# Score products and two weight heads moved in front of a data-dependent branch, with the first rows of maxima loaded there

## The chip, the core and the metric

The kernel runs on one core of a Trainium2 chip. The core has a matrix engine (TensorE, PE in the profile), a vector engine (VectorE, DVE), an activation engine (ScalarE, ACT), a general engine (GpSimd, POOL) and an engine that mostly issues transfers (SyncE, SP), besides 16 DMA engines. Each engine works through its own queue of instructions in order, and semaphores hold an instruction back until its inputs are there. The metric is the device time of one execution in microseconds (us).

## The reference

The input is layer-normalised once; an attention with 32 heads of 16 and one shared key and value head (A), and a layer of experts chosen by product keys (B), are added to the input.

```python
x = A_x                                   # 1 x 2048 x 512
xn = _layernorm(x, axis=-1)
# A
q = (xn @ wq).reshape(B, S, 32, 16).transpose(0, 2, 1, 3)
k, v = xn @ wk, xn @ wv
p = softmax(einsum("bhqd,bkd->bhqk", q, k) * 16 ** -0.5)
a = einsum("bhqk,bkd->bhqd", p, v) ... @ wo
# B: 32 heads, 64 x 64 experts, two of them per head and token
s1 = einsum("nhd,ed->nhe", q1, k1); s2 = einsum("nhd,ed->nhe", q2, k2)
# the best 2 of each, the best 2 of their 4 sums, softmax g over these
act = gelu(einsum("nd,nhkd->nhk", xn, u[top_e]))
b = einsum("nhk,nhk,nhkd->nd", g, act, v[top_e])
return x + a + b
```

## The kernel before, in words

**Tiles.** The 2048 tokens are 16 tiles of 128, in four groups of four. For the experts a "chunk" is four of the 32 heads: its score product for one tile of tokens is a 128x512 result of twelve matmuls over four slices of the model dimension and three terms of a split of both operands into a high and a low part (`item`, line 531). Eight maxima (line 544) and eight index searches (line 546) on VectorE follow for each such item. Four items are a batch; `batch` works out the gates on VectorE and ScalarE and the expert numbers on GpSimd (lines 590 to 606).

**Weights of a chunk.** `wp_make(c)` forms the folded weights of a chunk: one step for each of four heads (load of `wqt`, line 471; a few matmuls, line 487; a copy on ScalarE, line 488), then four steps of transposes (line 494) with a high part from ScalarE (line 496) and a low part from VectorE (line 497).

**One thread of score work.** `score_thread` yields the whole score work in small steps, each with a cost in us: 0.9 for a head, 0.45 for a slice of transposes, 0.705 for three matmuls of an item. `run_scores(until=...)` runs steps until the account `spent` reaches a value, `run_scores(key=...)` until the expert numbers of one item exist. Chunk 0's weights are 4 x 0.9 + 4 x 0.45 = 5.4 in this account.

**Gathers.** `gather` fetches, for one slot of 128 tokens, the rows of both expert tables by an indirect transfer from GpSimd's queue (line 987) into one of twelve buffers (`NGB`). `dot` (line 999) then forms the activation on VectorE, and `add` (line 1034) adds the weighted row to the sum of the tile. A buffer is free again after its `add`.

**The start.** Group after group is normalised (`norm_group`, with a square root on ScalarE, line 154), transposed (`transpose_group`, lines 182 to 187), projected to keys and values (`project_kv`) and to queries (`project_q`, lines 229 to 241, twelve matmuls for each of four slices, the results stored to memory by SP). Here the framework's own scheduler orders each engine's instructions: the order in the code is a priority, and what is ready may go ahead. Between the key projection of group 1 and the rest stand the weights and the four items of chunk 0 with their maxima, and then `flush`, which runs the deferred work (the exponential of the gates, line 583, among it). The first six gathers stand after group 2's keys, the next six after group 3's.

**The guard.** `guard` (lines 252 to 267) bounds the scores of the attention from the largest squared norms of queries and keys: a few small operations on VectorE, two one-column transposes on TensorE (`pm`, line 258), and a flag (line 264). Every engine loads the flag (line 265) and branches on it (line 266). Only if the bound is exceeded does `true_maxima` run, which works out the real maxima into the memory tensor `d_m`; with these inputs it does not, and `d_m` holds the zeros that `zero_m` wrote.

**The loop.** Behind it, 256 steps and some more run with an order written out by hand for all engines (`manual_schedule`). A step `d` takes two key blocks of an attention unit: scores (line 327), exponentials (line 330), products with the values (line 341). In `mid` come dots, sums and deferred work, in `fill` score steps up to the target `aim`, which rises from `done0`, the account at the loop's start, to 948 in equal shares. `pos` counts how many dots should have been formed; it starts at 0.0 and grows by 2.1 in the first steps and by other rates later, and in the last quarter by what is left divided by the steps that are left. `load_q(u)` loads a unit's query rows (lines 317 to 319) and, with `maxima`, its two rows from `d_m` (line 314). In the very first step `load_q(0, rows=False)` loads the rows of maxima for unit 0, behind the branch, and `run_scores(until=spent[0] + 1.8)` starts chunk 1's weights.

The calls of the start are at the bottom of the kernel (lines 1203 to 1260).

Of the kernel before, what the change touches and what calls it, by code (L numbers as in the profile page):

```python
# [40 lines left out]
NGB = 12  # L41
# [14 lines left out]
def tile_kernel(ctx, tc, x, wq, wkv, wo, wqT, kT, uv, ub, vb, out):  # L56
# [194 lines left out]
    def guard():  # L251

        mm = small.tile([P, 2], F32, name="mm", bufs=1)
        nc.vector.reduce_max(mm[:, 0:1], qmax, axis=AX.X)
        nc.vector.reduce_max(mm[:, 1:2], ksq_p, axis=AX.X)
        p = xtile("pm")
        for i in range(2):
            nc.tensor.transpose(p[:1, i * P:(i + 1) * P], mm[:, i:i + 1], ident)
        m2 = small.tile([1, 2], F32, name="m2", bufs=1)
        nc.vector.reduce_max(m2, p[:1, :2 * P].rearrange("p (a n) -> p a n", a=2), axis=AX.X)  # L260
        pr = small.tile([1, 1], F32, name="prd", bufs=1)
        nc.vector.tensor_mul(pr, m2[:, 0:1], m2[:, 1:2])
        fl = small.tile([1, 1], I32, name="flag", bufs=1)
        nc.vector.tensor_scalar(fl, pr, LIMIT2, None, op0=OP.is_gt)
        flag = nc.values_load(fl[0:1, 0:1], min_val=0, max_val=1)
        with tc.If(flag != 0):
            true_maxima()

    def true_maxima():
        ptile = lambda dt, shape: late[0].tile(list(shape), dt, name="mx", tag="pt", bufs=6)  # L270
# [34 lines left out]
    def load_q(u, rows=True, maxima=True):  # L305
        qb, hg = units[u]
        qa = qa_bufs[u % 2]
        QA[u] = qa
        c = slice(qb * 512, (qb + 1) * 512)
        for b in range(2):  # L310
            h0 = 4 * hg + 2 * b
            o = 64 * b
            if maxima:
                nc.sync.dma_start(raw(qa[o + 48:o + 50]), d_m[:, h0:h0 + 2, c])
            if rows:
                src = [d[h0 * DH:(h0 + 2) * DH, c].rearrange("(h r) n -> r h n", r=DH) for d in (d_qh, d_ql)]
                nc.sync.dma_start(raw(qa[o:o + 16]), src[0])
                nc.sync.dma_start(raw(qa[o + 16:o + 32]), src[0])
                nc.sync.dma_start(raw(qa[o + 32:o + 48]), src[1])
# [756 lines left out]
    def posts():  # L1076
        while POST:
            for fn in POST.pop(0):
                fn()
# [48 lines left out]
    spent = [0.0]  # L1128

    def run_scores(until=None, key=None):  # L1130
        while (until is not None and spent[0] < until) or (key is not None and key not in IDX):
            posts()
            try:
                cost = next(sgen)
            except StopIteration:
                spent[0] = 1e9
                posts()
                return
            if cost is None:

                if key is None:
                    return
                continue
            spent[0] += cost
# [4 lines left out]
    def att_steps(d, mid, fill):  # L1149
        i = 2 * d  # L1150
        run(STORES)
        if 144 <= i < STEPS and i % 128 == 16:
            PWO.extend((i // 128 - 1, j) for j in range(4))
        if i < STEPS:
            u, kc = divmod(i, 16)
            if i == 0:
                load_q(0, rows=False)
                run_scores(until=spent[0] + 1.8)
            if kc == 4 and u + 1 < 32:
                load_q(u + 1)  # L1160
            scores(u, kc, 0)
            scores(u, kc, 1)
        if 0 < i <= STEPS:
            pu, pk = divmod(i - 2, 16)
            pv(pu, pk)
            pv(pu, pk + 1)
            if pk == 14:
                unit_tail(pu)
        mid()
        if i < STEPS:  # L1170
            scores(u, kc + 1, 0)
            scores(u, kc + 1, 1)
        if out_ready() and (i % 128 >= HOLD and PWO[0][0] != 1 or i % 128 >= 32 and i % 4 == 0 and PWO[0][0] == 1):
            block_out()
            spent[0] += 3.6
        fill()

        pp, r = divmod(i, 32)
        if pp and pp < 16:
            if r == 4:  # L1180
                pair_load(pp - 1)
            if r == 6:
                pair_invert(pp - 1)
            if r == 10:
                pair_spread(pp - 1)
            if r == 12:
                pair_tail(pp - 1)
        if i == STEPS - 4:
            for j in range(3):
                last_out_a(j)  # L1190
        if i == STEPS + 2:
            last_out_a(3)
            last_out_b()
        if i >= 124 and i % 128 == 124 or i == STEPS - 30:
            lent[0] = 2
        if 128 <= i < STEPS and i % 128 == (26 if i // 128 == 2 else 10) or i == STEPS - 10:
            load_wo()
        if i == STEPS - 6:
            load_last()
# [29 lines left out]
    for base in (48, 112):  # L1229
        nc.scalar.dma_start(raw(kaug[base:base + 2, :]).rearrange("r (i n) -> r i n", n=512),  # L1230
                            ones_f[:, None, :].to_broadcast([2, 4, 512]))
    run_scores(key=(0, 0, 3))
    flush()
    zero_m()
    norm_group(2, xs[2])
# [1 line left out]
    transpose_group(2)  # L1237
    project_kv(2)
    xs.append([load_x(3 * GT + j, False) for j in range(GT)])
    gathers(NGB // 2)  # L1240
    project_q(2, wqs)
    norm_group(3, xs[3])
    transpose_group(3)
    project_kv(3)
    gathers(NGB // 2)
    project_q(3, wqs)
    run(STORES)
    start_stack.close()
    wp_load(1, 0)
    wp_load(1, 1)  # L1250
    late[0] = pool("late", bufs=1)
    load_q(0, maxima=False)
    guard()
    E_ = mybir.EngineType
    with tc.manual_schedule(engines={E_.PE, E_.Activation, E_.DVE, E_.Pool, E_.SP}):
        done0 = spent[0]
        half = STEPS // 2
        pos, since = 0.0, half
        for d in range(half + 24):


            if dense_on[0] != 0:
                since = d
            if dense_on[0] == 1:
                pos += 2.6 if d < half * 3 // 4 else max(0.0, NSL - pos) / max(half - 3 - d, 1)
            else:
                pos += (2.1 if len(IDX) < NC * TPH else 2.3 if 0 <= d - since < 12 else 1.75, 0, 1.4, 1.5, 0.5)[dense_on[0]]

            todo = max(min(int(pos + 0.001), g_next[0]) - d_next[0], 0)

            def mid():
                post = POST[:]
                POST.clear()
                for act, _ in post:
                    act()
                tanhs(d_next[0])
                run(ON_ACT)
                ON_ACT.extend(LATER_ACT)
                LATER_ACT.clear()
                run(LAST)  # L1280
                LAST.extend(LATER)
                LATER.clear()
                rest = BEHIND[:]
                BEHIND.clear()

                dots(d_next[0] + todo - 1)
                if a_ready[0] > a_next[0]:
                    weigh(a_next[0] // SB)
                dots(d_next[0] + 1 if todo > 0 else 0)
                for _, fn in post:  # L1290
                    fn()
                sums = min(a_ready[0] - a_next[0], max(todo, 3) if d < half else 4)
                if dense_on[0] > 2:
                    sums = min(sums, 2)
                if quiet[0] > 0:
                    quiet[0] -= 1
                    sums = 0
                if dense_on[0] == 2:
                    run(CHAIN)

                def go():
                    n = sums
                    while rest or CHAIN or n > 0:
                        if n > 0:
                            adds(1)
                            n -= 1
                        elif not rest:
                            run(CHAIN)
                        if CHAIN:
                            CHAIN.pop(0)()  # L1310
                        if rest:
                            rest.pop(0)()
                    gathers(4)

                    for _ in range(1 if d < half - 4 else NT):
                        if OUTS:
                            experts_out(OUTS.pop(0))

                if dense_on[0] == 2:
                    POST_FILL.append(go)  # L1320
                else:
                    go()

            aim = done0 + (FILL - done0) * (d + 1) / half if d < half else 1e6

            def fill():
                run_scores(until=min(aim, spent[0] + MOST))
                run(POST_FILL)

            att_steps(d, mid, fill)  # L1330
        flush()
        run(STORES)
        while a_next[0] < NSL:
            dots(NSL)
            run(CHAIN)
            tanhs(d_next[0])
            adds(SB)
            run(STORES)
            gathers(NGB)
        assert not OUTS  # L1340
        run(STORES)
# [37 lines left out]
```

## Time and profile before

| what | value |
|---|---|
| median of three runs | 1915.05 us (1909.74 to 1916.33) |
| the profiled execution's own time | 1918.82 us |
| its span in the trace | 1917.1 us |
| granted clock of TensorE, mean | 0.985 |
| bytes read and written in memory | 426.49 MB and 55.61 MB |
| transfers by indirect gathers | 268.47 MB in 73728 packets |
| first two score products of the loop | from 139.21 us |

The span is divided into 40 slices of about 48 us; a digit gives the busy share of a slice in tenths (9 is 90% or more), and the row PEclk the granted clock in tenths. A row of the timeline has the start and length in us, engine and line, what is written from what, how often, and in brackets the idle time before it with what ended that. Rows whose engine ends in q are those of a queue, not of its engine. The profile does not count a register load, a branch or an issued transfer as busy time.

### The profile page before, as it was taken

The numbers are of one execution on the slowest core, as the hardware profiler recorded it, in microseconds if no ns is written. First come the engines' busy times: TensorE is split into PE (matmuls) and PEld (weight loads), VectorE is DVE, ScalarE is ACT, GpSimd is POOL, SyncE is SP. The second block draws the span as 40 slices with busy tenths as digits, with TensorE's granted clock in tenths as the row PEclk, the third lists the DMA queues.
The fourth block names the chain that finished last, engine by engine and source line by source line (L and its number), as shares of the span: only waits on it lengthen the run. The fifth ranks groups of instructions, "written<-read, shape, count | busy, mean of one in ns | idle before, by whom it ended". The sixth has DMA issues, their size and how long they took to land.

```text
span 1917.1 us, 35007 instructions
## 1 busy us (share of the span) xinstructions
PE 1822.9 (95%) x10990; PEld 961.5 (50%) x10990; DVE 1633.0 (85%) x6381; ACT 1290.6 (67%) x1803; POOL 693.8 (36%) x920
## 2 busy tenths in 40 slices
PE   6879999999999889999999999999998899999998
PEld 4544444555555344555555454555543345555553
DVE  6626888889998987999999797899989779999994
ACT  3236666655557987787877555555579777878773
POOL 1202334334443213343444354344522124444430
PEclk9989999999999999999999999999999899999999
DMA  7856878898673678898999987877646878899982
GB/s 264 312 191 235 293 267 289 286 296 282 232 261 111 223 245 259 250 288 274 284 289 307 340 283 234 290 244 264 229 129 220 263 222 292 267 285 280 295 265 79
DMA packets 245724, 489.76 MB, mean 255 GB/s; under 512 B 93972, under 2 KB 106644, under 8 KB 245532
## 3 DMA queue, kind: packets, MB, share of 16 engines
q0 software_dynamic: 73728, 268.47, 42.1%
q1 hardware_dynamic: 170568, 218.18, 35.0%
q8 instruction: 88, 1.44, 0.3%
q10 hardware_dynamic: 1236, 0.82, 0.1%
q14 instruction: 104, 0.85, 0.1%
HBM read 426.49 MB, written 55.61 MB: 251 GB/s over the span
## 4 chain that ended last, share of the span: by engine, by line
PE 76%; DVE 10%; DMA 3%; ACT 2%; issue 1%; SPq 1%; ACTq 0%; DVEq 0%
PE pv L341 20%; PE psc L531 18%; PE sc L327 15%; PE pact L733 9%; PE pout L872 9%; DVE oh L792 3%; PE pwo L434 2%; DVE xa L1034 2%; DVE g L999 1%; PE pw L487 1%; DVE oh L795 1%; ACT pt L330 1%; DVE oh L794 1%; DMA wqt<-in_wqT_dram 1%; DMA wk<-dw 1%
## 5 line engine op out<-in xcount | busy, mean ns | idle before, releaser
L330 ACT ACTIVATE pt<-sc 128x1024 f32<-128x1024 f32 x1024 | 994.6, 1028 | 449.1 <-PE sc L327 394.2
L987 POOL DMA_INDIRECT g<-in_uv_dram,idx x512 | 555.0, 1084 | 997.1 <-DVE xa L1034 518.3
L341 PE MATMUL pv<-pt,vaug 128*32 128x512 f32 x4096 | 499.4, 604 | 0.0
L327 PE MATMUL sc<-qa,kaug 64*128 64x512 f32 x2048 | 387.7, 451 | 15.7 <-ACT pt L330 14.1
L531 PE MATMUL psc<-wk,xt 128*128 128x512 f32 x1536 | 390.4, 402 | 8.0 <-DMA wk<-dw 4.4
L1034 DVE SCALAR_TENSOR_TENSOR xa<-g,w,xa 128x512 f32<-128x512 f32 x512 | 372.2, 745 | 0.1
L999 DVE CUSTOM_DVE_ANT_0 g<-g,xa 128x512 f32<-128x512 f32 x512 | 335.7, 682 | 6.2 <-DMA g<-in_uv_dram,idx 6.2
L531 PEld LDWEIGHTS psc<-wk,xt 128*128 128x128 f32 x1536 | 278.9, 189 | 111.8 <-issue 39.6
L327 PEld LDWEIGHTS sc<-qa,kaug 64*128 64x128 f32 x2048 | 157.4, 186 | 332.3 <-ACT pt L330 206.5
L341 PEld LDWEIGHTS pv<-pt,vaug 128*32 128x32 f32 x4096 | 107.7, 110 | 247.6 <-issue 246.0
L546 DVE FIND_INDEX8 i<-m,psc 128x8 uint32<-128x64 f32 x1024 | 206.6, 222 | 0.0
L733 PE MATMUL pact<-xt,wk 128*128 128x512 f32 x768 | 196.0, 400 | 0.0
L872 PE MATMUL pout<-wk,wd 128*128 128x512 f32 x768 | 194.9, 402 | 0.2 <-DVE wd L930 0.2
L544 DVE MAX8 m<-psc 128x8 f32<-128x64 f32 x1024 | 146.6, 215 | 41.3 <-PE psc L531 36.8
L872 PEld LDWEIGHTS pout<-wk,wd 128*128 128x128 f32 x768 | 140.8, 188 | 47.5 <-DVE act L999 5.5
L733 PEld LDWEIGHTS pact<-xt,wk 128*128 128x128 f32 x768 | 139.4, 188 | 48.5 <-issue 17.4
L875 DVE TENSOR_TENSOR da<-da,pout 128x512 f32<-128x512 f32 x128 | 82.9, 680 | 10.1 <-PE pout L872 6.6
L698 DVE TENSOR_TENSOR wk<-rw,wk 128x512 fp32r<-128x512 f32 x128 | 84.9, 684 | 6.7 <-ACT wk L697 6.7
L792 DVE TENSOR_TENSOR oh<-oh 128x2048 f16<-128x2048 f16 x64 | 78.0, 1219 | 0.6 <-ACT pt L330 0.4
L697 ACT CAST wk<-rw 128x512 fp32r<-128x512 f32 x128 | 74.1, 632 | 0.0
L546 DVE MATCH_VALUE_LOAD i<-m,psc 128x8 f32 x1024 | 72.6, 71 | 0.0
L1022 DVE SCALAR_TENSOR_TENSOR w<-gth,ga 128x4 f32<-128x4 f32 x128 | 20.5, 160 | 51.2 <-ACT gth L1015 50.6
(159 smaller groups left out, 1344.6 us busy)
## 6 DMA issues: line engine op xcount, KB each, us to landing
wk<-dw SPq DMA_DIRECT2D x96, 512.0 KB
wqt<-in_wqT_dram SPq DMA_DIRECT2D x32, 512.0 KB
dw<-wk SPq DMA_DIRECT2D x32, 512.0 KB
rw<-in_ub_dram SPq DMA_DIRECT2D x64, 256.0 KB
rw<-in_vb_dram SPq DMA_DIRECT2D x64, 256.0 KB
gy<-dg SPq DMA_DIRECT2D x64, 256.0 KB
qa<-dqh SPq DMA_DIRECT2D x128, 64.0 KB
g<-in_uv_dram,idx POOLq DMA_INDIRECT x512
```

The lines of the kernel that those rows point to most:

```text
L327: nc.tensor.matmul(p[:, b, :], kaug[o:o + 64, kc * P:(kc + 1) * P], QA[u][o:o + 64, i, :], start=True, stop=True)
L330: nc.scalar.activation(pt, p, AF.Exp, scale=SCALE)
L341: nc.tensor.matmul(PV[u][32 * j:32 * j + 32, :], vaug[:, kc, :], pt[:, b, :], start=kc == 0, stop=kc == 15)
L531: nc.tensor.matmul(p, XT[k][:, a, j * P:(j + 1) * P], WC[n_][k][:, bb, :], start=n == 0, stop=n == 11)
L544: nc.vector.max(m8[:, jb, s, :], p[:, s * E:(s + 1) * E])
L546: nc.vector.max_index(i8[:, jb, s, :], m8[:, jb, s, :], p[:, s * E:(s + 1) * E])
L733: nc.tensor.matmul(p, us[:, a, k * P:(k + 1) * P], XT[k][:, c, :], start=n == 0, stop=n == 11)
L792: nc.vector.tensor_tensor(out=oa, in0=num(P), in1=bc(0, tb, P), op=OP.is_equal)
L872: nc.tensor.matmul(p, wd[0][:, a, j * P:(j + 1) * P], vs[:, c, :], start=n == 0, stop=n == 5)
L987: nc.gpsimd.indirect_dma_start(out=gt, out_offset=None, in_=uv, in_offset=bass.IndirectOffsetOnAxis(ap=IDX[ph, c, ti][:, s:s + 1], axis=0))
L999: nc.vector.tensor_tensor_reduce(u, u, XN[TPH * ph + ti], scale=1.0, scalar=0.0, op0=OP.mult, op1=OP.add, accum_out=a[:, i:i + 1])
L1034: nc.vector.scalar_tensor_tensor(acc, v, w[:, i:i + 1], acc, op0=OP.mult, op1=OP.add)
```

## The change

Four items of chunk 0 leave their place after group 1's keys; there, `run_scores(until=5.3)` now stops when chunk 0's weights are made. The items, their deferred work, all twelve gathers and the first heads of chunk 1's weights stand in `guard`, after the flag has been computed and ahead of the load of it. `load_q(0)` loads the rows of maxima along with the query rows ahead of the guard; where the branch is taken, they are loaded again behind `true_maxima`. The first loop step no longer does either, and `pos` starts at -2.1.

```diff
@@ guard
         nc.vector.tensor_scalar(fl, pr, LIMIT2, None, op0=OP.is_gt)
+        run_scores(key=(0, 0, 3))
+        flush()
+        gathers(NGB)
+        run_scores(until=spent[0] + 1.8)
         flag = nc.values_load(fl[0:1, 0:1], min_val=0, max_val=1)
         with tc.If(flag != 0):
             true_maxima()
+            load_q(0, rows=False)
@@ att_steps
             u, kc = divmod(i, 16)
-            if i == 0:
-                load_q(0, rows=False)
-                run_scores(until=spent[0] + 1.8)
             if kc == 4 and u + 1 < 32:
@@ the start
-    run_scores(key=(0, 0, 3))
+    run_scores(until=5.3)
     flush()
...
-    gathers(NGB // 2)
     project_q(2, wqs)
...
     project_kv(3)
-    gathers(NGB // 2)
     project_q(3, wqs)
...
-    load_q(0, maxima=False)
+    load_q(0)
     guard()
...
-        pos, since = 0.0, half
+        pos, since = -2.1, half
```

## The prediction

> **What bounds the kernel now.** I read the page's first two parts, then the start stage by stage, because the diff touches only what stands around the branch ahead of the attention loop.
>
> ```profile
> span 1917.1 us, 35007 instructions
> PE 1822.9 (95%) x10990; PEld 961.5 (50%) x10990; DVE 1633.0 (85%) x6381; ACT 1290.6 (67%) x1803; POOL 693.8 (36%) x920
> ...
> PE   6879999999999889999999999999998899999998
> ...
> PEclk9989999999999999999999999999999899999999
> ```
>
> TensorE is busy 95% of the span and has its loose slices at the very start. So time can only come out of places where TensorE waits, and those are here (the windows view; columns are length, busy time of each engine with instruction counts, granted clock, DMA share):
>
> ```profile
> 52.20:63.15 10.95, 10.95 (x50) 9.02 (x49) 9.07 (x74) 0.55 (x1) 0.00 (x0) 1.00 0.74 281
> 63.15:76.69 13.54, 10.49 (x44) 7.27 (x42) 10.16 (x55) 6.80 (x11) 8.02 (x16) 1.00 0.76 257
> 76.69:104.30 27.61, 21.66 (x85) 13.79 (x85) 10.20 (x20) 6.39 (x12) 5.52 (x6) 0.88 0.86 335
> 104.30:124.73 20.43, 19.18 (x87) 12.46 (x86) 8.48 (x14) 7.98 (x15) 0.00 (x0) 1.00 0.61 226
> 124.73:133.72 8.99, 0.96 (x4) 0.09 (x3) 2.24 (x6) 0.94 (x2) 0.00 (x0) 0.63 0.26 90
> 133.72:139.21 5.49, 4.68 (x13) 1.09 (x14) 0.00 (x0) 1.17 (x2) 0.00 (x0) 0.68 0.64 222
> 139.21:147.42 8.21, 5.45 (x22) 2.05 (x20) 0.42 (x1) 7.12 (x9) 0.00 (x0) 0.80 0.37 111
> ...
> 139.21:1917.10 1777.89, 1718.81 (x10558) 895.74 (x10556) 1559.73 (x6133) 1248.69 (x1728) 672.26 (x875) 0.99 0.78 255
> ```
>
> The first row is chunk 0's score products, the second the rest of query projection 1, the third all of group 2, the fourth all of group 3, the fifth the guard with its branch, the sixth the first heads of chunk 1's weights, the seventh the first loop step. Groups 2 and 3 do the same work, yet group 2 takes 7.18 us more (27.61 against 20.43). The guard has 0.96 us of TensorE work in 8.99. From the first loop score (139.21) on, TensorE is busy 1718.81 of 1777.89 us, so the loop keeps nearly all of what it gets early or late: a shift of the first score is a shift of the end.
>
> Now the timeline of group 2 (start, length, instruction, and in brackets the idle time before it and what released it):
>
> ```profile
> 66.16 0.32 POOL L590 CAST fi<-i 128x64 f32<-128x64 uint32 x1 [57.50 <-DVE i L546]
> ...
> 68.79 1.28 ACT L583 ACT_TABLE_LOAD   x1
> 68.92 1.16 POOL L987 DMA_INDIRECT g<-in_uv_dram,idx  x1 [0.29 <-POOL idx L606]
> ...
> 72.51 1.28 ACT L154 ACT_TABLE_LOAD   x1
> ...
> 74.39 0.69 DVE L999 CUSTOM_DVE_ANT_0 g<-g,xa 128x512 f32<-128x512 f32 x1 [3.00 <-DMA g<-in_uv_dram,idx]
> ...
> 76.38 0.38 PE L237 MATMUL pqs<-qsq,blk 128*32 128x512 bf16 x1 [1.83 <-DVE act L999]
> ...
> 82.66 0.69 DVE L241 TENSOR_REDUCE qmax<-pqs 128x1 f32<-128x512 f32 x1 [3.03 <-remote]
> 82.80 0.94 POOL L987 DMA_INDIRECT g<-in_uv_dram,idx  x1 [0.30 <-remote]
> 86.17 1.07 ACT L183 CAST xtt<-ptr 128x512 fp32r<-128x512 f32 x2 [6.77 <-remote]
> ...
> 86.81 1.36 PE L200 MATMUL pkv<-xtt,wkv_h 128*32 128x512 f32 x2 [4.91 <-ACT xtt L183]
> ```
>
> The twelve gathers are issued from 68.92 to 83.74. While they fill the DMA engines, ScalarE stands still for 6.77 us and VectorE for 3.03 us, released by something that the view calls only "remote", and TensorE loses 4.91 us waiting for ScalarE. After it the matmuls are slow (1.36 us for two), so the clock adds to it. Nothing like it is in group 3, which has no gathers. Two loop dots (line 999) ran at 74.39 although the code has them behind the branch: outside the written order the framework's scheduler lets work cross the branch.
>
> The guard itself:
>
> ```profile
> 126.48 0.38 PE L237 MATMUL pqs<-qsq,blk 128*32 128x512 bf16 x1 [1.75 <-ACT qsq L236]
> 127.83 0.58 PE L258 MATMUL pm<-ident,mm 128*1 128x128 f32 x2 [0.98 <-DVE mm L254]
> 129.09 0.14 DVE L264 TENSOR_SCALAR flag<-prd 1x1 int32<-1x1 f32 x1
> ```
>
> What its two lines did in each queue (duration in ns as least, median, most, then first and last start):
>
> ```profile
> L265 PEldq TENSOR_LOAD <-flag x1: 492/492/492, 129.3 to 129.3; - x1
> L266 POOLq COMPARE_BRANCH  x1: 45/45/45, 129.8 to 129.8; - x1
> L266 PEldq COMPARE_BRANCH  x1: 3568/3568/3568, 129.9 to 129.9; - x1
> ```
>
> The weight heads before and behind it, again in the timeline:
>
> ```profile
> 45.41 3.65 PE L487 MATMUL pw<-wqt,kTs 128*64 128x512 f32 x14
> ...
> 133.75 3.67 PE L487 MATMUL pw<-wqt,kTs 128*64 128x512 f32 x8 [5.33 <-PEq L266]
> ...
> 134.39 5.28 SPq L471 DMA_DIRECT2D wqt<-in_wqT_dram  x4
> ...
> 138.20 1.08 PE L487 MATMUL pw<-wqt,kTs 128*64 128x512 f32 x4 [0.78 <-PE pw L487]
> ...
> 139.92 1.28 ACT L330 ACT_TABLE_LOAD   x1
> ```
>
> The flag is written at 129.23. TensorE's queue loads it (0.49 us), spends 3.57 us in the branch and starts again at 133.72: 4.49 us. Then come three heads (twelve matmuls; four make a head), not the two that the step of 1.8 names, since the sum of costs falls a rounding short of its bound.
>
> **The change part by part.** Negative is saved time on the path to the first score.
>
> a. Chunk 0's 48 score matmuls leave the stretch 52.20 to 63.15 and come back behind group 3. They cost 10.95 us in either place: 0 by themselves. VectorE's 32 maxima and 32 index searches move along; an item's round is 60.62 minus 57.90, 2.72 us, against 10.95/4 = 2.74 us on TensorE, so they keep pace and end one item behind.
>
> ```profile
> 57.90 1.15 DVE L544 MAX8 m<-psc 128x8 f32<-128x64 f32 x8
> ...
> 60.62 1.15 DVE L544 MAX8 m<-psc 128x8 f32<-128x64 f32 x8
> ```
>
> b. Query projection 1 loses the dots, the searches on VectorE and the two table loads (68.79 and 72.51) between its steps. Its stretch idles 13.54 minus 10.49 = 3.05 us; group 3's idles 1.25. Saving between 0 and 3.05; I take 1.5, near the difference of 1.8.
>
> c. Group 2 without the gathers: between 0 (the stall has another cause) and 7.18 (it becomes group 3). I take 6, near group 3, because the stall starts and ends with the burst.
>
> d. The flag's latency, 124.73 to 129.23, is 4.50 us with 0.96 us of work; the score products fill the 3.5. Between 0 (they are put elsewhere) and 3.5; I take 3.5, for 10.95 us are ample cover and wait for nothing here.
>
> e. The three heads cost 5.49 us behind the branch, with half the clock and SP's loads (134.39) queued behind the branch. In front of it, at the rate of 45.41, they cost 12 x 3.65/14 = 3.1: saving 2.4 at most, 0 at worst. The loads are hidden under the score products. If that cover is gone, the third head waits as at 138.20. I take 2.4.
>
> f. TensorE's load and branch stay: the same 4.3 us (0.49, 3.57 and the step after), now behind the heads instead of behind the flag. I take 0; at worst the fetch meets the burst, below.
>
> g. The exponential's table is loaded for chunk 0's gates in front of the branch and no square root comes after it, so the load at 139.92 is gone: between 0 and 1.3; I take 1.3. The maxima rows' two small transfers leave SP's queue behind the branch and cost nothing in front of it, under the score products.
>
> h. The twelve gathers now start when the indices of chunk 0 are there: after VectorE's last item and POOL's chain of 2.76 us (66.16 to 68.92), some 5.5 us behind the last product, while TensorE is in its branch. POOL's own branch stands behind them. The first rows are there 74.39 minus 68.92 = 5.5 us later, and the start position of -2.1 gives the first step no dots, so the dots of the second step, about 8.2 us on (seventh row), find their rows. What can be lost is the stall of c, at its new place: 0 to 7.18. I take 2.5: nearer to 0, since DMA share there is 0.37, where the stall met 0.86.
>
> i. VectorE leaves its branch later, so chunk 1's weight halves come later: 0 to 2.7 (one item); I take 0.5. The two dots that move into the loop meet an idle VectorE (0.42 of 8.21 us busy) and cost 0; the schedule spreads the rest of the lag over its last quarter. The cost account begins 2.7 higher and changes only how the fill is spread.
>
> Sum: -1.5 - 6 - 3.5 - 2.4 - 1.3 + 2.5 + 0.5 = -11.7 us. From the profiled execution's 1918.8 us (its span of 1917.1 and 1.7 around it) that is 1907.1. The three runs shown have a median of 1915.05, 3.8 lower, so on their footing the forecast is **1903.4**.
>
> A page of the Trainium skill speaks against a part of this: "TensorE: Matmul & The Clock Gate", section "Part 1: The HAM clock gate (the "warmup" mystery)", has the array go to half its clock after about 3.4 us idle and need as long of work to come back. The clocks of 0.63 and 0.68 in the fifth and sixth row agree. By it the branch's gap still leaves a cold array, now in front of the scores: half of 3.4 us, 1.7, would be lost of e, as an estimate from that page, and the sum would be -10.0.
>
> **The rivals.** *The burst only moves.* The stall of c turns up behind the branch with its whole price: the sum has +7.2 in place of +2.5, -7.0 in all, and 1908.1. For it: the same twelve transfers, and several engines leaving a branch at that moment. Against it: loop steps all have gathers, and they run nearly without TensorE waiting.
> Of the Trainium skill, "Runtime: NRT & Kernel Launch", section "Instruction fetch mechanics", says that a taken branch to code not yet held must fetch it by DMA; by that rule the branch and the burst compete for the same engines. The branch's 3.57 us agree, though no row shows that fetch under load.
>
> *The order does not change as written.* The scheduler let dots cross the branch; it can also pull products and gathers forward into the gaps of groups 2 and 3. Then b, c and d are not had, h costs nothing, and e and g remain: -3.7, 1911.4. Against it: the code's order is its priority, and projections fill TensorE in groups 2 and 3 (19.18 of 20.43).
>
> *The branch is a meeting point (slower).* If no engine can leave the branch before all have entered it, TensorE waits for POOL, which stands behind twelve gathers. Counted from the last product: 2.7 (VectorE's item), 2.8 (index chain), 14.8 (68.92 to 83.74) make 20.3, against 3.1 for the heads: 17.2 us more. Then the sum is -14.7 + 0.5 + 17.2 = +3.0, and +9.0 if group 2's stall also stays; its middle, +6, gives 1921.1. It decides once the wait exceeds 14.2 us. For it: the present trace has all engines idle at the branch, so it could not show. Against it: each queue has its own load and its own branch of 45 ns, TensorE's alone being long.
>
> **How the numbers follow.** Forecast 0.60, with a range of its own from 1897 (every saving whole and no loss: 3.05 + 7.18 + 3.5 + 2.4 + 1.3 = 17.4) to 1909; the burst only moves 0.12; order unchanged 0.12; meeting point 0.16. A measurement of this kernel can tell about 0.3% from no change, 5.7 us: 1909.3 to 1920.8. Faster: 0.60 of the forecast, less its slow edge, with two thirds of the second, a little of the third, about 0.70; same 0.14; slower 0.16. The range reaches over the second and third case and leaves out the meeting point: 1895 to 1914.
>
> **What would show it.** Group 2's stretch near 20.4 us without a "remote" wait; line 531's first 48 products between the last projection and line 266; ScalarE with two table loads in the start instead of four; twelve line 487 matmuls ahead of the branch; the first score near 126 us; TensorE still about 4 us in the branch; from there to the end the same 1778 us. I would be wrong if the gathers come before the guard in the trace, if TensorE's branch lasts as long as POOL's gathers, or if the stretch behind the first score grows by more than the first score is earlier.

## The result: the first score came 9.2 us earlier, and the end 18 us later

The changed kernel takes 1932.01 us (median of six runs, 1927.93 to 1937.30), the kernel before 1914.28 us (six runs, 1909.74 to 1918.59): a ratio of 1.0098, 95% interval 1.0079 to 1.0117. (Here and below the ratio is estimated from all runs of both kernels; it is not quite the quotient of the two medians.) It is slower by 17.7 us; 1903.4 us, a gain of 11.7, was forecast. Line numbers of the changed kernel are 5 higher behind the guard, those of e12 below 6.

The page of the changed kernel, parts 1 and 2:

```profile
span 1927.9 us, 34996 instructions
...
PE 1823.1 (95%) x10990; PEld 962.0 (50%) x10990; DVE 1632.9 (85%) x6381; ACT 1289.7 (67%) x1801; POOL 686.9 (36%) x920
...
PE   6979999999998889999999899999988899999998
...
PEclk9989999999999999999999899999999999999999
```

TensorE does the same work in the same busy time (1823.1 against 1822.9 us). What grew is its idle time, and the digits show no place for it at the start: new eights stand in the later slices.

The windows view of the changed kernel's start, cut at the same events as in the prediction (rest of query projection 1 with the last transposes of the weights, group 2, group 3, the flag's latency, chunk 0's products, heads and branch, the first loop step):

```profile
52.10:65.91 13.81, 13.80 (x64) 9.96 (x64) 6.89 (x12) 6.29 (x11) 0.00 (x0) 1.00 0.52 173
65.91:85.23 19.32, 18.57 (x85) 12.49 (x84) 11.38 (x26) 6.87 (x13) 0.00 (x0) 1.00 0.64 238
85.23:105.65 20.42, 19.45 (x87) 12.47 (x86) 8.58 (x14) 8.09 (x15) 0.00 (x0) 1.00 0.66 251
105.65:108.98 3.33, 0.51 (x3) 0.14 (x3) 1.54 (x3) 0.94 (x2) 0.00 (x0) 1.00 0.98 376
108.98:121.67 12.69, 12.69 (x51) 10.05 (x49) 8.77 (x75) 0.00 (x0) 0.00 (x0) 0.87 0.88 286
121.67:129.98 8.31, 2.84 (x13) 0.71 (x13) 4.26 (x34) 3.14 (x5) 4.10 (x12) 0.98 0.36 103
129.98:140.35 10.37, 8.91 (x35) 4.43 (x35) 1.98 (x3) 6.10 (x8) 7.93 (x9) 0.68 0.97 342
```

The first score is at 129.98 instead of 139.21. But from there to the end of the span it is 1927.9 - 130.0 = 1797.9 us, against 1777.9 before:

```profile
129.98:1927.90 1797.92, 1720.53 (x10556) 896.26 (x10556) 1560.31 (x6137) 1248.30 (x1726) 674.90 (x885) 0.99 0.78 255
```

Twenty microseconds were lost behind the part that the change moved. This is the last of the signs of being wrong that the prediction had named: the stretch behind the first score grew by more than the first score is earlier.

The 9.2 us come from one pair of executions, and the start varies. In the six kernels whose start is that of before (before, e4, e5, e11, e13 and e14 below) the first score comes at 135.2 to 139.2 us, in the changed kernel and e1, e7, e8 and e10, which have its start, at 128.3 to 130.2. On average it is 8.0 us earlier.

To find where, the start of the first exponential of each loop step was read from both traces (the instructions of line 330 and line 335 in order of time, four to a step). The first column is its time in the profile of before in us, the others are the difference to it: the changed kernel, and five kernels of the experiments below.

```
step   before   changed    e1     e7     e4     e11     e5
   0    141.2    -10.2   -11.1  -10.0   -1.7   -0.8   -3.4
   1    147.1     -2.9   -10.4   -9.5   +2.6   -2.9   -2.7
   6    184.5     -0.7    -9.8   -9.2   +2.3   +4.7   -2.6
  28    351.1     -4.3    -7.7   -9.8   -1.2   +9.4   -1.0
  64    600.3     +0.0    -8.0  -10.1   +1.2  +10.7   -1.1
  76    666.7     +1.2    -2.9  -10.1   +4.8  +15.0   +3.6
 104    854.8     +6.6    -3.5   -9.8  +11.9  +12.6   +3.3
 132   1051.6     +6.7    -3.0   -9.9  +11.2  +12.6   +5.5
 140   1112.6    +10.8    -5.9  -11.0  +14.3  +16.6   +6.2
 188   1440.7     +9.4    -6.0  -11.1  +12.7  +21.3   +6.6
 200   1507.3     +9.7    -1.2  -12.0  +13.3  +19.8  +10.6
 255   1894.8    +12.2    +0.8  -13.1  +13.5  +18.1  +11.8
```

The profiled execution of before lies above the median of its runs (1918.8 against 1914.28 us), and its first score is the latest of the six equal starts, so all columns flatter the other kernels by a few us; how a column changes from row to row is what counts. In the changed kernel's column the lead of 10.2 us shrinks to 2.9 within the first step, is gone by step 64, and turns into a lag of 6.6 by step 104 and of 10.8 at step 140. The experts of two of the four token groups are not gathered but worked out by matmuls over all experts with one-hot rows (lines 825, 733 and 872); a stretch of steps in which these run is called a dense phase here. In the trace of before the first fills steps 63 to 134 and the second steps 181 to 253. Steps 64 to 104 lie in the first, and steps 132 to 140 hold its end.

The largest wait of TensorE in the loop is there. The timeline of the changed kernel around it, of SP, VectorE and TensorE (rows picked):

```profile
1050.71 1.69 SPq L510 DMA_DIRECT2D wk<-dw  x2
...
1053.07 0.59 SPq L379 DMA_DIRECT2D rc<-dsum  x1
...
1068.25 0.35 DVE L384 RECIPROCAL rc<-rc 128x32 f32<-128x32 f32 x1 [9.78 <-DMA rc<-dsum]
...
1071.78 2.13 PE L877 MATMUL pout<-wk,wd 128*128 128x512 f32 x4 [8.78 <-DVE wd L935]
```

The same transfers in the timeline of the kernel before:

```profile
1046.82 0.32 SPq L374 DMA_DIRECT2D rc<-dsum  x1
...
1049.16 0.91 SPq L505 DMA_DIRECT2D wk<-dw  x2
```

Before, the small load of a pair's softmax sums (16 KB) was issued ahead of the next chunk's weights; after, behind them. VectorE stands 9.78 us at the reciprocal of these sums, the split of the gated rows is queued behind it, and TensorE waits 8.78 us for that split. No instruction of the diff is anywhere near.

### The profile page after: what moved, and what is told of

Its sections match the earlier page's. It is cut to its first block, busy times and chain, and to the rows that moved or that the text cites. A ratio compares the mean times of both kernels' runs of the same rounds, so it can differ in the third digit from the quotient of the medians.

```text
span 1927.9 us, 34996 instructions
## 1 busy us (share of the span) xinstructions
PE 1823.1 (95%) x10990; PEld 962.0 (50%) x10990; DVE 1632.9 (85%) x6381; ACT 1289.7 (67%) x1801; POOL 686.9 (36%) x920
## 4 chain that ended last, share of the span: by engine, by line
PE 72%; DVE 12%; DMA 3%; issue 2%; ACT 2%; POOL 1%; SPq 0%; another core or an unknown queue 0%; ACTq 0%; DVEq 0%; POOLq 0%
PE pv L346 19%; PE psc L536 18%; PE sc L332 14%; PE pout L877 8%; PE pact L738 8%; DVE oh L797 3%; DVE xa L1039 2%; PE pwo L439 2%; DVE g L1004 2%; PE pw L492 1%; DVE oh L800 1%; ACT pt L335 1%; DVE oh L799 1%; DMA rc<-dsum 1%; DMA g<-in_uv_dram,idx 1%
## 5 line engine op out<-in xcount | busy, mean ns | idle before, releaser
L738 PEld LDWEIGHTS pact<-xt,wk 128*128 128x128 f32 x768 | 139.9, 188 | 47.7 <-issue 16.4
L595 POOL CAST fi<-i 128x64 f32<-128x64 uint32 x32 | 8.8, 273 | 185.2 <-DVE i L551 184.2
```

What stands on the lines that cost most here:

```text
L738: nc.tensor.matmul(p, us[:, a, k * P:(k + 1) * P], XT[k][:, c, :], start=n == 0, stop=n == 11)
```

## The experiments

All ratios are to runs of the kernel before on the same chip.

**e1: the target line led back.** The changed kernel runs the three heads ahead of the loop, so the account at the loop's start, from which the line of targets rises, is 2.7 higher.

```diff
-        done0 = spent[0]
+        done0 = spent[0] - 2.7
```

> The changed kernel with the target line of the fill started 2.7 lower (done0 less the three heads), as it was before the change. Theory A (the account: the line starts higher by the three heads, so the dense phases meet the attention's small transfers at another moment, and the 7 us lost in steps 60 to 104 and the 4 us lost in steps 132 to 136 come from that): 1932 falls by 8 to 12 us, to 1920 to 1924, and the wait of TensorE for the gated rows of 8.8 us near step 134 is gone. Theory B (the dots start one step later, and that lag does it): no change, 1930 to 1934. Theory C (only the burst of twelve gathers at the loop's entry costs time): no change, 1930 to 1934.

Measured: 1921.49 us against 1911.64, ratio 1.0062 (1.0043 to 1.0081). Beside the 1.0098 of the change that is about 0.36%, 7 us. In the table the first step keeps its lead (-10.4 instead of -2.9), and the 8.78 us are gone. Theory A holds in part: the line costs, but the lead still melts from 8.0 to 2.9 us between steps 64 and 76 and from 6.0 to 1.2 between steps 188 and 200.

**e2: the count of dots led back.**

```diff
-        pos, since = -2.1, half
+        pos, since = 0.0, half
```

> The changed kernel with the count of dots started at 0.0 instead of -2.1, so that the first step forms two dots again. Theory A: no change, 1930 to 1934, or a few us more because the first dots wait for their rows. Theory B: falls by 8 to 12 us, to 1920 to 1924. Theory C: no change.

Measured: 1933.97 us, ratio 1.0111 (1.0088 to 1.0134): no gain, but for a reason that none of the theories named. TensorE's waits from 120 to 145 us, and what the branch did in VectorE's queue (ns, then start):

```profile
PE sc L332 <- DVEq L270: 16.7, 1, 16.7
```

```profile
L270 DVEq COMPARE_BRANCH  x1: 72/72/72, 134.5 to 134.5; - x1
L270 DVEq EVENT_SEMAPHORE  x1: 21/21/21, 140.8 to 140.8; - x1
```

The scheduler again pulled the two dots in front of the branch. Their rows were not there, VectorE came to its branch only at 134.5, was out of it at 140.8, and the first score waited 16.7 us for that. So the branch is a meeting point, though with VectorE and not with POOL. What VectorE waited for behind its branch can be inferred from the times of the trace's DMA packets: a packet of 8 KB in the queue named "instruction" starts at 138.96 us, 4.45 us behind the branch, while the gathers are being issued, and lands 1.6 us before 140.8; in the changed kernel the one that fits VectorE starts 1.0 us behind its branch. This is what the -2.1 prevents, and so this run's time says nothing on theory B.

**e4: the line alone, on the kernel before.**

```diff
-        done0 = spent[0]
+        done0 = spent[0] + 2.7
```

> The kernel before with the target line alone started 2.7 higher; nothing is moved. Theory A: 1914 rises by 8 to 12 us, to 1922 to 1926, without any move across the branch. Theories B and C: no change, 1912 to 1917.

Measured: 1931.26 us, ratio 1.0102 (1.0085 to 1.0120). With nothing moved, one number in the schedule costs as much as the whole change. The wait for the gated rows appears here too; TensorE's waits over the loop of e4 (total, times, longest in us):

```profile
PE pg L825 <- DVE oh L795: 28.2, 28, 2.4
...
PE pout L872 <- DVE wd L930: 7.9, 2, 7.7
```

In the kernel before these two are 21.4 us and 0.2 us:

```profile
PE pg L825 <- DVE oh L795: 21.4, 28, 1.6
```

```profile
PE pout L872 <- DVE wd L930: 0.2, 1, 0.2
```

**e5: the dots alone, on the kernel before.**

```diff
-        pos, since = 0.0, half
+        pos, since = -2.1, half
```

> The kernel before with the count of dots alone started at -2.1; nothing is moved. Theory B: 1914 rises by 8 to 12 us, to 1922 to 1926. Theories A and C: no change, 1912 to 1917.

Measured: 1929.19 us, ratio 1.0099 (1.0081 to 1.0117). A lag of two dots, 1.4 us of VectorE, costs a percent as well. Its column loses 4.7 us between steps 64 and 76 and 4.0 between 188 and 200: the same places as in e1, which has the same lag. Both of these fall in dense phases, where the one-hot products of line 825 run. So theories A and B do not exclude each other, as both had it: each counter alone costs 18 to 20 us, more than the 8 to 12 expected of it.

**e8: the lag caught up, the line as changed.** The two dots are formed in steps 3 and 5, behind the entry.

```diff
         for d in range(half + 24):
+            if d in (3, 5):
+                pos += 1.05
```

> The changed kernel with the missing two dots formed in steps 3 and 5, the target line as changed. Theory A+B: some of 1932 is had back, 3 to 8 us, to 1924 to 1929, and what is left over before is the line's. Theory A alone (the line carries all): 1930 to 1934.

Measured: 1927.49 us against 1909.59, ratio 1.0091 (1.0068 to 1.0114). Of the change's 0.98% only 0.07% are had back, within both intervals. The time lies in the range that theory A+B gave only because the kernel before ran 5 us faster on this chip than in the first comparison; the ratio is that of theory A alone. So the two costs do not add: where the line is shifted, the dots' lag matters little; alone on the kernel before they cost 1.02% and 0.99%.

**e7: both led back.** The edits of e1 and e8 together. Compared line by line, the order of instructions on TensorE is that of the kernel before from the first score on; on ScalarE it is from 180 us on, on VectorE from 197 us on.

> The changed kernel with both schedules led back to those of before: the target line starts 2.7 lower, and the two dots that the first step lacks are formed in steps 3 and 5 (1.05 each). The moved work of the start stays moved. Theory A+B (both lags cost, each by itself, and the start's gain is real): the traces showed step 20 earlier than before by 9.7 us with the line led back, and nothing is left to lose it: 1902 to 1909, faster than before by 0.3 to 0.6%. Theory D (the moved gathers or the loop's new entry cost time all along the loop, whatever the schedules): 1915 to 1922, as with the line alone led back.

Measured: 1902.56 us (12 runs, 1899.06 to 1909.54) against 1909.59 (23 runs), ratio 0.9963 (0.9949 to 0.9976). The whole of the moved work, with the loop's order led back, is **faster than before**. Its column stays between -8 and -13 us throughout, and from the first score to the end it takes no longer than the kernel before (1777.9 us):

```profile
130.19:1903.30 1773.11, 1714.54 (x10556) 894.84 (x10556) 1559.52 (x6137) 1247.30 (x1726) 684.11 (x885) 0.99 0.79 259
```

The gain of 7.0 us is nearly the 8.0 by which the first score is earlier on average. Theory A+B holds and D falls: with the order held, neither the moved gathers nor the new entry shows a cost along the loop.

**e9: four gathers in front of the branch**, on e7.

```diff
-        gathers(NGB)
+        gathers(4)
```

> The kernel with both schedules led back, and four gathers instead of twelve in front of the branch; the rest follow four a step in the loop. If the burst at the loop's entry costs time (theory C): 2 to 5 us faster than with twelve. If it does not: the same within 2 us; if the loop then runs short of rows: slower by some us.

Measured: 1905.65 us, ratio 0.9969 (0.9954 to 0.9984), the same as e7 within its interval. But the edit did not thin the burst: POOL issues the other eight without a pause behind the four. The first of the twelve starts at 127.45 us (127.39 in e7), and the twelfth in e9:

```profile
141.87 0.94 POOL L992 DMA_INDIRECT g<-in_uv_dram,idx  x1 [0.30 <-PE pwt L499]
```

and in e7:

```profile
141.39 0.94 POOL L992 DMA_INDIRECT g<-in_uv_dram,idx  x1 [0.30 <-PE pwt L499]
```

So this run does not test theory C. What speaks against a lasting cost of the burst is e7 itself, which has it whole and loses 0.5 us in its first step.

**e10: the reciprocal one step later**, on the changed kernel.

```diff
-            if r == 6:
+            if r == 8:
                 pair_invert(pp - 1)
```

> The changed kernel with the reciprocal of a pair's sums (pair_invert) one step later, at 8 instead of 6 of a unit pair's 32. Theory E (the 8.8 us that TensorE waits near step 134 come from VectorE standing at a reciprocal whose sums were asked for behind bulk transfers, which happens because the higher target line ends the dense phase there one fill earlier): that wait is gone, and 1932 falls by 3 to 5 us, to 1926 to 1930. If the wait has another cause: it stays and the time is 1930 to 1934.

Measured: 1943.29 us against 1916.57, ratio 1.0134 (1.0113 to 1.0155): slower than the changed kernel's 1.0098 too, though the two intervals just touch. TensorE's waits over the loop of e10:

```profile
PE psc L536 <- DMA wk<-dw: 6.9, 2, 5.9
PE pout L877 <- DVE gy L920: 6.2, 2, 3.4
```

The wait of 8.78 us is gone, as expected, but at the same place TensorE now waits 5.9 us for the next chunk's weights, and by step 104, far ahead of that place, the kernel is already 14.1 us behind the one before, where the changed kernel is 6.6 behind. What was shown is the way of that wait; that its removal is worth its length was a miss.

**e11, e13, e14: the line of the kernel before shifted by -2.7, +0.9 and -0.9.**

```diff
-        done0 = spent[0]
+        done0 = spent[0] - 2.7
```

> The kernel before with its target line 2.7 lower, nothing else. Theory F (it is the earlier score work that costs): 1905 to 1913, the same or faster. Theory G (the loop of before sits at an alignment that any shift spoils): slower than before by 8 to 20 us, 1918 to 1930.

> The kernel before with its target line 0.9 higher (one head, a third of the shift of the change). Theory G (the loop of before sits at an alignment that any shift spoils, whatever its size): slower by 0.4 to 1.0%, as with 2.7. Theory I (the cost grows with the size of the shift): slower by 0.2 to 0.4%, a third of the 1.0% of 2.7.

> The kernel before with its target line 0.9 lower. Theory G: slower by 0.4 to 1.0%. Theory I: slower by 0.2 to 0.4%, a third of the 0.9% of -2.7.

Measured: 1.0088 (1.0065 to 1.0110), 1.0043 (1.0020 to 1.0065) and 1.0059 (1.0041 to 1.0076). With e4 that is a curve with its lowest point at the kernel before: +0.9% and +1.0% at -2.7 and +2.7, +0.6% and +0.4% at a third of that. Theory F falls: it does not matter that score work comes earlier, only that it comes at another moment. Between G and I the runs do not decide cleanly: the cost grows with the shift, but by far less than in proportion.

**e12: two items ahead of the guard's transposes**, on e7.

```diff
+        run_scores(until=spent[0] + 5.6)
         p = xtile("pm")
```

> The kernel with both schedules led back, and two of the four items written ahead of the guard's two transposes. Theory H (TensorE's queue is in order, so the products written behind the transposes could not cover the 4 us between the last query product and the transposes): these 4 us are filled and the clock does not fall, the first score comes 3 to 5 us earlier and the time is 3 to 5 us below the 1902.6 of the same kernel without it. If the way to the first score is VectorE's, not TensorE's: no more than 1 us.

Measured: 1909.07 us against 1916.57, ratio 0.9965 (0.9949 to 0.9980), no better than e7's 0.9963. The products now start at 105.1 instead of 109.1 us, but the first score is at 129.8 in place of 130.2 us. The rows of e12's entry (start, length, instruction):

```profile
119.35 1.12 DVE L550 MAX8 m<-psc 128x8 f32<-128x64 f32 x8
...
121.78 1.28 ACT L589 ACT_TABLE_LOAD   x1
...
123.61 1.08 PE L493 MATMUL pw<-wqt,kTs 128*64 128x512 f32 x4 [2.48 <-ACT ex L589]
```

and TensorE's branch there:

```profile
L271 PEldq COMPARE_BRANCH  x1: 4228/4228/4228, 124.2 to 124.2; - x1
```

VectorE's last maxima start at 119.35, 2.6 us earlier than in e7 (121.92). But then the third head waits 2.48 us for ScalarE, which loads the exponential's table in between, and TensorE's branch lasts 4.23 us where e7's lasts 3.41. Nor is TensorE's own branch the last wait. These are the semaphore instructions with which SP and TensorE leave the branch, and the first score:

```profile
L271 SPq EVENT_SEMAPHORE  x8: 3/17/717, 129.2 to 129.7; - x8
...
L271 PEldq EVENT_SEMAPHORE  x1: 51/51/51, 128.5 to 128.5; - x1
```

```profile
129.80 1.32 PE L333 MATMUL sc<-qa,kaug 64*128 64x512 f32 x4 [5.11 <-DMA wqt<-in_wqT_dram]
```

VectorE is out at 127.5 and TensorE at 128.5, but the score starts at 129.80. The row names a transfer as its releaser; the operands of the instructions point to SP, which at 129.70 sets a semaphore that TensorE waits for at that moment. SP's first instruction behind its branch (125.2) comes 4.0 us later. The 4 us filled in one place are lost again to the next waits on the way: theory H falls, and the way to the first score is not VectorE's alone either.

## Why the prediction was wrong, step by step

The forecast's gain was right in kind and too large in the start; the loss came from a step that it had put at nothing.

- **The step that failed** is in i: the dots' lag that "the schedule spreads" and the cost account that "changes only how the fill is spread". Taken alone on the kernel before, the account costs 1.02% (e4) and the lag 0.99% (e5); led back together they turn the change from +0.98% to -0.37% (e7). With them falls the premise that "a shift of the first score is a shift of the end": it holds for a shift in time, but not where the order of the loop changes with it.
- **a** was 0 and became a loss of 1.7 us in this execution: the products lasted 12.69 us instead of 10.95. They start behind a stretch of 3.33 us with 0.51 us of work, and the granted clock there is 0.87. The rule that the prediction weighed, of the Trainium skill, "TensorE: Matmul & The Clock Gate", section "Part 1: The HAM clock gate (the "warmup" mystery)", half the clock after about 3.4 us idle and for about as long, agrees with this row: half of 3.4 us is 1.7. The prediction applied it to the scores and not to the products. The same stretch does not always bring the loss: e7, e8 and e10 have it (rows of 12.8 us), e1 and e9 do not (11.2 us, at a clock of 1.00):

```profile
109.64 11.17 PE L536 MATMUL psc<-wk,xt 128*128 128x512 f32 x48
```

- **b**, 1.5 us, came with 2.9 us and was lost again ahead of its place. From group 1's first transposes to group 2's it was 76.69 - 31.61 - 10.95 = 34.1 us before and 65.91 - 31.80 = 34.1 us after. Of this the part behind the fourteen head matmuls of chunk 0's weights (line 487, from 45.41 us before and 48.53 after) shrank from 20.3 to 17.4 us, and the part ahead of them, with group 1's key projection, grew from 13.8 to 16.7. There TensorE waits longer for the squares of the queries, before:

```profile
39.19 0.38 PE L237 MATMUL pqs<-qsq,blk 128*32 128x512 bf16 x1 [1.17 <-ACT qsq L236]
```

  and after, where ScalarE makes two copies of query slices ahead of the square:

```profile
40.84 0.51 PE L237 MATMUL pqs<-qsq,blk 128*32 128x512 bf16 x1 [2.63 <-ACT qsq L236]
```

  The granted clock from 31.80 to 52.10 us is 0.92, before it was 1.00. All eight kernels with the changed start show the longer wait, none of the six others does. The diff does not touch these lines: the framework's scheduler ordered them otherwise, and why is not shown.

- **c**, 6 us, came: group 2 went from 27.61 to 19.32 us, with no "remote" wait. That is 8.29 us, more than the upper bound of 7.18. In the six kernels with the gathers in groups 2 and 3 the two groups together take 44.4 to 47.7 us, in the changed kernel 39.4, so the gathers cost 5.0 to 8.3 us there. The price has more than one form: e4 and e5 have no "remote" wait in group 2, but in group 3 the copies of the queries wait 7.2 and 9.7 us for the stores of earlier ones.
- **d**, 3.5 us, is the term that was over-sized in the start. That the products "wait for nothing here" overlooked that TensorE's queue is in order: the products are written behind the two transposes, which wait for the last maximum of the queries. The first idle part, 3.33 us, stayed; only what lies behind the transposes, about 1.2 us, is covered. The rows:

```profile
108.85 0.38 PE L258 MATMUL pm<-ident,mm 128*1 128x128 f32 x2 [1.07 <-DVE mm L254]
108.98 12.76 PE L536 MATMUL psc<-wk,xt 128*128 128x512 f32 x48
```

- **e**, 2.4 us, came: 2.84 us for the heads instead of 5.49.
- **f** was 0 and cost about 1 us. The first score does not wait for TensorE's own branch alone. TensorE was out of it at 127.8, but started at 129.98, released by VectorE, which has the last searches and the gates in front of its own branch (SP's semaphore instructions, at 129.1 to 129.7, end just ahead of it, so a faster VectorE alone would have gained 0.3 us at most, an estimate from these times):

```profile
L270 PEldq EVENT_SEMAPHORE  x1: 51/51/51, 127.8 to 127.8; - x1
...
L270 DVEq EVENT_SEMAPHORE  x1: 21/21/21, 129.9 to 129.9; - x1
...
129.98 1.31 PE L332 MATMUL sc<-qa,kaug 64*128 64x512 f32 x4 [5.47 <-DVEq L270]
```

  The meeting point was written down as a rival, with POOL as the late one and 1921.1 us. POOL passes its branch at 129.5, with two of its twelve gathers in front of it and ten behind, although the code has all twelve in front; so its price did not apply. The prediction spoke against the rival with each queue's own branch of 45 ns; but the next instruction of VectorE comes 2.9 us behind its branch. With VectorE late (e2) the first exponential is at 142.0 instead of 131.0 us.
- **g**, 1.3 us, came with 0.95: the exponential follows the first score by 1.05 instead of 2.00 us.
- **h**, a loss of 2.5 us, is there in some executions and not in others. The changed kernel's first step has a "remote" wait of ScalarE, 4.37 us, under the burst:

```profile
143.44 0.58 ACT L501 CAST wk<-pwt 128x512 fp32r<-128x512 f32 x1 [4.37 <-remote]
```

  e10, with the same entry, has it too (4.43 us); e1, e7 and e8 have the burst without the wait. The first step of the changed kernel loses 7.3 us, that of e10 7.2. That of e8, which has the same higher line and so the same longer fill (16 transposes and six products, where e7 runs four transposes), loses 4.0, and those of e1 and e7 lose 0.7 and 0.5 (all read as in the table above). So about 4 us of the 7.3 go with the longer fill, a cost of the line that i had put at nothing, and about 3 with the wait.

The start was to be earlier by 13.4 us and was earlier by 9.2. Its parts: -8.29 (c), -1.17 (d), -2.65 (e), +1.74 (a), +0.98 (f) and +0.16 from the rest, b among it.

What stays open is why the dense phases cost more at every other alignment. One wait was followed to its end (the pair's sums behind the weights). The others are many small ones, such as the 6.8 us more that TensorE waits for the one-hot rows in e4, and no single mechanism was shown for them. That wait alone does not go with the loss: it is 25.9 us in e7, which is fast, and 20.1 in e5, which is slow.

## What to carry to other kernels

Where a loop's order is generated from counters (work done, dots formed), a change ahead of the loop also changes the counters' start values, and so the order of everything behind it. Hold the generated order fixed when a start is changed, compare the two orders, and only then judge the change: here that turned +0.98% into -0.37%. Work put in front of a branch to hide a latency can hide it only where it stands ahead, in each in-order queue, of the instruction that waits; and behind a branch that all engines take, work starts when the latest engine that it depends on is through (VectorE in the changed kernel and e2, SP in e12). Where a scheduler orders the instructions, an edit can change that order far from its place, as in b, and an experiment's edit has to be found in the trace before its time is read, as e9 shows.

## What the runs showed of the hardware

- A branch not into the conditional part cost TensorE's queue 3.4 to 4.2 us in these runs, and it did not shrink when other work stood around it. On the other queues the branch itself is 45 to 72 ns, but VectorE's next instruction follows 2.9 to 3.1 us later (126.9 to 129.9 in the changed kernel) and SP's 2.5 to 4.4, and VectorE's 6.3 us later in e2 (134.5 to 140.8), where the gathers were being issued. POOL's follows 0.2 us later.
- By the times of the DMA packets, a load of code stands behind this. In all fourteen traces a packet of 16 KB of a DMA queue named "instruction" lands while TensorE is in its branch, 1.4 to 1.5 us before its next instruction, and one of 8 KB lands 1.4 to 1.6 us before VectorE's next instruction. The latter starts 1.0 us behind VectorE's branch in thirteen of them, and 4.45 us behind it in e2. Which engine a packet serves is inferred from these times.
- ScalarE and VectorE can stand still for 3 to 7 us under a burst of gathers (6.77 and 3.03 us before, 4.37 in the changed kernel), released by something the profile does not name. The same burst passes without it in e1, e7 and e8. A load of code is not what ended it in the changed kernel: no packet of the instruction queues starts between 131.9 and 150.7 us there, and the wait ends at 143.44.
